# Zero rows under the first products and dummy products between them, in a fused mLSTM and mixture-of-experts kernel

## The chip, the core and the metric

The kernel runs on one core of one Trainium2 chip. Its engines work side by side, each through its own list of instructions in order: TensorE (PE in the profile; PEld is its weight load), VectorE (DVE), ScalarE (ACT), GpSimd (POOL) and SyncE (SP, which here only issues DMAs). The metric is the time on the device in microseconds (us), the median of several runs; lower is better.

## What is computed

An mLSTM attention over 4 batches, 8 heads, 768 positions and head size 40, then a dense layer with a squared ReLU, then a layer in which each token goes to one of 8 experts:

```python
# attention, for each step t (k, v, q of that step; gates i and f)
m_new  = maximum(f + m, i)
f_stab = exp(f + m - m_new);  i_stab = exp(i - m_new)
C = f_stab * C + i_stab * (v k^T);  n = f_stab * n + i_stab * k
y[t] = sigmoid(o) * (C q) / maximum(|n . q|, 1)
# x: 3072 tokens of 320, from y
x = maximum(x @ w_in, 0)**2 @ w_out                       # w_in 320 x 2048
# expert layer: e = argmax(x @ w_gate), p = softmax(x @ w_gate)[e]
out = p * (maximum(x @ w1[e], 0) @ w2[e])                 # w1 320 x 1024
```

All of it is float32.

## The kernel before

The 768 positions of each batch are cut into 6 chunks of 128, 24 chunks in all. Within a chunk the recurrence becomes matrix products: scores of keys against queries (`scores`, L743, tiles `sp`), weighted with the decays of the gates (`Ab`) and multiplied with the values (`values`, L752, tiles `pv`), plus the state `C` of the chunks before, read with the queries (`triples`, L708, tiles `tp<-C,q`) and updated with keys and values (tiles `tp<-vw,kvo`). The result is transposed (`across`, L717, tiles `xpt`) and split into a high and a low part (L725 to L727), since the dense layer works with float32 numbers as pairs of a high part that PE multiplies in one pass and a rest. Three chunks make a group of 384 tokens; for each group the dense layer runs over 16 slices `f` of its 2048 columns: eight products into `hp` (`l1`, L817), the squared ReLU on ACT and DVE, nine products into `acc` (`l2`, L846 to L848). The expert layer follows from about 578 us on.

One chunk is a generator, `main(n)`, of eight steps that end with `yield`. Its first six are advanced by the letter `h` of a string, `PLAN` (L62), its last two (transpose and split) by `y`. Other letters of the string load and unpack the weights of the dense layer (`A`, `R`, `T`, `W`, `H`, `L`; on ACT, DVE and POOL, L519 to L570), prepare the next chunk (`q`, `k`, `d`, `x`, `e`, `v`, `r`), advance the gates (`g`) and emit the dense layer (`l`, `s`, `m`). The code runs through the string once; that sets the order of every engine's instructions. The letter `h` stands 20 times ahead of the first `l`, the first products into `hp`; these steps reach into the fourth chunk. `nl[0]` counts the `l` emitted so far.

The gates of all chunks are turned into running sums `A`, on 36 rows (4 batches of 9), by two scans on DVE (`gate_stage`, L457 and L465). For chunk 0 the decays come from PE: `decays_first` adds a mask `neg`, by a product with the identity (L641), and then, head by head, row `2h + j` of `A`, picked out by a product with a matrix `sel` of 36 rows (L644). Then `columns` transposes three tables of the gates (L483, tiles `pt`) into `cT`, `wT` and `eAT`. Later chunks get their decays by DMA (L631).

For the first seven chunks (`WHOLE = 7`) keys and queries are loaded as 40 rows each and multiplied as float32, in several passes of PE (each such product has two records in the trace). From the eighth chunk on the product has 120 rows, which hold high and low parts of the same numbers, and one pass. The tiles `st` for them have 120 rows in both cases and rotate through two buffers.

`ones` is a tile of 128x128 bf16 ones that POOL fills at the beginning (L859). `acc0` is the PSUM bank of the dense layer's first accumulator. It is not used before the first `m`.

Of the kernel before, what the change touches and what calls it, by code (L numbers as in the profile page):

```python
# [9 lines left out]
F32 = mybir.dt.float32  # L10
# [7 lines left out]
ACTF = mybir.ActivationFunctionType  # L18
# [5 lines left out]
B, H, S, D = 4, 8, 768, 40  # L24
L = 128
NCH = S // L
HB = H + 1
HR = B * HB
# [24 lines left out]
XC_DVE = 2  # L53
FETCH = 2
PERIOD = 6

WHOLE = 7
KVO = 3
# [307 lines left out]

@with_exitstack
def kernel(ctx, tc, qk, q3, kvo, gates, w_in, w_out, wg, w12, cst, out, dbg=None):
    nc = tc.nc
    dbg = dbg or {}  # L370
# [6 lines left out]
    def pool(name, bufs, to, **kw):  # L377
        p = tc.tile_pool(name=name, bufs=bufs, **kw)
        to.append(p)
        return p.__enter__()  # L380
# [5 lines left out]
    ps2 = pool("ps2", 1, early_ps, space=PSUM)  # L386
# [4 lines left out]
    ident = cs[:, 0:128]  # L391
# [22 lines left out]
    xt = ctx.enter_context(tc.tile_pool(name="xt", bufs=2))  # L414
# [3 lines left out]
    at1 = pool("at1", 1, brief, side="right")  # L418
    at2 = pool("at2", 2, brief, side="right")
# [14 lines left out]
    def gate_stage():  # L434

        fi = scr[0:HR, 0:2 * S]
        nc.sync.dma_start(out=fi, in_=gates)
        f, i = fi[:, 0:S], fi[:, S:2 * S]

        sel = at1.tile([120, 2, H * L], F32, tag="kq", name="sel")[0:HR, 0].rearrange("p (h l) -> p h l", h=H)  # L440
        neg = at1.tile([128, H, 42], F32, tag="Y", name="neg").rearrange("p h d -> p (h d)")[:, 0:L]
        m = xt.tile([HR, S + 1], F32, tag="xh", name="m")
        a = xt.tile([HR, S], F32, tag="xh", name="a")
        A = xt.tile([HR, S], F32, tag="xl", name="A")
        c = xt.tile([HR, S], F32, tag="xl", name="c")
        msk = xrl.rearrange("p t n -> p (t n)")[0:HR, 0:S]
        wv, eA = msk, a
        yield
        nc.gpsimd.memset(msk, 1.0)
        nc.gpsimd.memset(msk.rearrange("p (c l) -> p c l", l=L)[:, :, 0:1], 0.0)  # L450
        nc.vector.memset(m[:, 0:1], -1e30)
        nc.gpsimd.memset(neg, 0.0)
        nc.gpsimd.affine_select(out=neg, in_=neg, pattern=[[1, L]], compare_op=ALU.is_ge, fill=-1e30, base=0, channel_multiplier=-1)
        nc.scalar.activation(out=sel, in_=ident[0:HR, 0:H].rearrange("p (h o) -> p h o", o=1).to_broadcast([HR, H, L]), func=ACTF.Copy)
        chunks[0].rows = (sel, neg, A)
        yield
        nc.vector.tensor_tensor_scan(out=m[:, 1:], data0=f, data1=i, initial=-1e30, op0=ALU.add, op1=ALU.max)  # L457
        yield
        nc.vector.tensor_tensor(out=a, in0=f, in1=m[:, 0:S], op=ALU.add)
        nc.gpsimd.tensor_tensor(out=c, in0=i, in1=m[:, 1:], op=ALU.subtract)  # L460
        yield
        nc.vector.tensor_tensor(out=a, in0=a, in1=m[:, 1:], op=ALU.subtract)
        nc.vector.memset(a[:, 0:1], 0.0)
        yield
        nc.vector.tensor_tensor_scan(out=A, data0=msk, data1=a, initial=0.0, op0=ALU.mult, op1=ALU.add)  # L465
        A3 = A.rearrange("p (c l) -> p c l", l=L)

        nc.sync.dma_start(out=A_d, in_=A)
        yield
        nc.vector.tensor_tensor(out=c, in0=c, in1=A, op=ALU.subtract)  # L470
        nc.scalar.activation(out=eA, in_=A, func=ACTF.Exp)
        yield
        nc.vector.tensor_tensor(
            out=wv.rearrange("p (c l) -> p c l", l=L),
            in0=c.rearrange("p (c l) -> p c l", l=L),
            in1=A3[:, :, L - 1:L].to_broadcast([HR, NCH, L]),
            op=ALU.add,
        )

        def columns(src, dst):  # L480
            pt = psa.tile([128, 512], F32, tag="a", name="pt")
            for ch in range(NCH):
                nc.tensor.transpose(out=pt[:, HR * ch:HR * ch + HR], in_=src[:, L * ch:L * ch + L], identity=ident[0:HR, 0:HR])  # L483
            nc.scalar.activation(out=dst, in_=pt[:, 0:HR * NCH].rearrange("p (c h) -> p c h", h=HR), func=ACTF.Copy)

        columns(c, cT)
        yield
        nc.scalar.activation(out=wv, in_=wv, func=ACTF.Exp)
        columns(wv, wT)
        yield  # L490
        columns(eA, eAT)
        eAL = const.tile([HR, NCH], F32, name="eAL")
        nc.vector.tensor_copy(out=eAL.rearrange("p (c o) -> p c o", o=1), in_=eA.rearrange("p (c l) -> p c l", l=L)[:, :, L - 1:L])
        nc.gpsimd.dma_start(out=L_d, in_=eAL)
        yield
# [88 lines left out]
    where = [divmod(n, 3) for n in range(NC)]  # L584
    first = [sum(GROUPS[:g]) for g in range(len(GROUPS) + 1)]
    xT = {}

    class Chunk:

# [13 lines left out]

        def qk(self):

            self.st = []
            for j in range(2):
                st = at2.tile([120, H * L], F32, tag="st", name="st")
                rows = D if self.n < WHOLE else 3 * D
                nc.sync.dma_start(out=st[0:rows], in_=qk[self.b, self.c, j, 0:rows])  # L610
                self.st.append(st)
            if self.c > 0:
                self.q3 = at2.tile([120, 3, L], F32, tag="q3", name="q3")
                nc.sync.dma_start(out=self.q3.rearrange("p g l -> p (g l)"), in_=q3[self.b, self.c])
# [19 lines left out]
        def decays_first(self):  # L634
            sel, neg, A = self.rows
            self.Ab = []
            self.Ap = []
            for j in range(2):
                self.Ab.append(at4.tile([128, 4, L], F32, tag="Ab", name="Ab"))
                self.Ap.append(psa.tile([128, 4, L], F32, tag="a", name="Ap"))  # L640
                nc.tensor.matmul(self.Ap[j], ident, neg.rearrange("p (o l) -> p o l", o=1).to_broadcast([128, 4, L]), start=True, stop=False)  # L641
            for j in range(2):
                for h in range(4):
                    nc.tensor.matmul(self.Ap[j][:, h], sel[:, 2 * h + j], A[:, 0:L], start=False, stop=(h == 3))  # L644
# [25 lines left out]
    chunks = [Chunk(n) for n in range(NC)]  # L670
# [19 lines left out]
    def ahead(m, name, *a):  # L690
        if (m, name, *a) not in over:
            over.add((m, name, *a))
            assert name != "decay" or m == 0 or (m, "causal", *a) in over
            log.append(LETTER[name])
            getattr(chunks[m], "decays_first" if (name, m) == ("decays", 0) else name)(*a)

    def more(name):

        for m in range(NC):
            for j in ((0,), (1,)) if name in ("causal", "decay", "round") else ((),):  # L700
                if name == "round" and m < WHOLE or (m, name, *j) in over:
                    continue
                return ahead(m, name, *j)
# [25 lines left out]
    def main(n):  # L729

        d = chunks[n]
        b, c, last = d.b, d.c, d.last
# [4 lines left out]
        def scores():  # L737
            for r in range(2):
                sps.append(psa.tile([128, 4, L], F32, tag="a", name="sp"))
            for h in range(H):  # L740
                c = slice(L * h, L * h + L)
                k, q = (d.st[j][0:D, c] for j in range(2)) if n < WHOLE else (d.kq[:, j, c] for j in range(2))
                nc.tensor.matmul(sps[h % 2][:, h // 2], k, q, start=True, stop=True)  # L743

        def weigh(r):
# [112 lines left out]
    ones = const.tile([128, 128], BF16, name="ones")  # L858
# [225 lines left out]
    def step():  # L1084
        n = steps[0] // PERIOD
        if n < NC:
            log.append("h")
            next(mains[n])
        steps[0] += 1

    def rest():

        n = tails[0]
        if n < NC and steps[0] >= PERIOD * (n + 1):
            log.append("y")
            if next(mains[n], "end") == "end":
                tails[0] += 1
# [14 lines left out]
    def evac(n):  # L1112

        return PERIOD * n + 8

    def half(n):

        if steps[0] < evac(n):
            n, h = divmod(steps[0], PERIOD)
            rest()  # L1120
            step()
            prepare(n, h)
# [5 lines left out]
    with tc.manual_schedule():  # L1128
# [4 lines left out]
        nl, nd = [0], [0]  # L1133
# [185 lines left out]
            letters[x] = lambda x=x: turn(x)  # L1319
        for name, x in LETTER.items():  # L1320
            letters[x] = lambda name=name: more(name)
        for word in PLAN:
            for x in word:
                if x in "tBS":
                    {"t": lambda: tick(1), "B": lambda: half(NC), "S": settle}[x]()
                else:
                    if x in "gcz":
                        log.append(x)
                    letters[x]()
        if ALL:  # L1330
            dbg.setdefault("log", []).append("".join(log))
# [135 lines left out]
```

## Time and profile before

| | |
|---|---|
| median of 3 runs | 792.76 us (791.84 to 796.58) |
| the profiled execution | 796.21 us, of which the span of its instructions 794.3 |
| PE busy | 745.2 us (94% of the span) |
| DVE, ACT, POOL busy | 506.8, 434.7, 362.2 us |
| chain of work that ended last, by engine | PE 76%, DVE 9%, DMA 5%, ACT 4%, issue 3%, POOL 1% |
| granted TensorE clock, mean over the span | 0.993 |

Busy times are sums over one engine. An engine's record of a product lasts from its start to its end in the array, and neighbours overlap, so a row's time for several is that of the whole run of them. The granted clock is the share of 2.4 GHz that the records of the clock tell of: 1.00 is 2.4 GHz, 0.50 is 1.2. The idle time in square brackets in a timeline row is that of the engine just before the row.

### The profile page before, as it was taken

The numbers are of one execution on the slowest core, as the hardware profiler recorded it, in microseconds if no ns is written. First come the engines' busy times: TensorE is split into PE (matmuls) and PEld (weight loads), VectorE is DVE, ScalarE is ACT, GpSimd is POOL, SyncE is SP. The second block draws the span as 40 slices with busy tenths as digits, with TensorE's granted clock in tenths as the row PEclk, the third lists the DMA queues.
The fourth block names the chain that finished last, engine by engine and source line by source line (L and its number), as shares of the span: only waits on it lengthen the run. The fifth ranks groups of instructions, "written<-read, shape, count | busy, mean of one in ns | idle before, by whom it ended". The sixth has DMA issues, their size and how long they took to land.

```text
span 794.3 us, 14262 instructions
## 1 busy us (share of the span) xinstructions
PE 745.2 (94%) x5075; PEld 730.6 (92%) x5075; DVE 506.8 (64%) x1169; ACT 434.7 (55%) x811; POOL 362.2 (46%) x430
## 2 busy tenths in 40 slices
PE   5676999999999999999999999999979999999996
PEld 3675999999999999999999999999979999999995
DVE  4674787677766677676568755363647555867553
ACT  5877796544653544553544543544246555866453
POOL 2775356554763455364345300423126444556640
PEclk9999999999999999999999999999999999999998
DMA  7575556444654445344345000100168665875620
GB/s 224 154 219 179 168 170 175 139 128 144 215 158 133 114 114 145 104 113 144 113 114 166 7 1 32 32 31 1 61 227 275 185 173 169 250 234 192 200 82 15
DMA packets 58822, 109.29 MB, mean 138 GB/s; under 512 B 7132, under 2 KB 36413, under 8 KB 58614
## 3 DMA queue, kind: packets, MB, share of 16 engines
q1 hardware_dynamic: 49542, 84.67, 36.6%
q10 hardware_dynamic: 5040, 11.82, 4.8%
q0 software_dynamic: 4160, 11.77, 4.5%
q8 instruction: 46, 0.75, 0.4%
q14 instruction: 34, 0.28, 0.1%
HBM read 99.37 MB, written 10.50 MB: 138 GB/s over the span
## 4 chain that ended last, share of the span: by engine, by line
PE 76%; DVE 9%; DMA 5%; ACT 4%; issue 3%; POOL 1%; ACTq 0%; SPq 0%; DVEq 0%; POOLq 0%
PE hp L817 21%; PE hp L282 12%; PE acc L846 6%; PE acc L848 6%; PE acc L847 6%; PE pv L752 4%; PE op L302 4%; PE op L301 4%; PE op L303 4%; DMA st<-in_qk_dram 3%; PE sp L743 2%; PE tp L708 2%; DMA raw<-in_w_in_dram 2%; PE lp L911 2%; PE xp L268 1%
## 5 line engine op out<-in xcount | busy, mean ns | idle before, releaser
L624 POOL TENSOR_TENSOR kq<-st,kq 120x256 fp32r<-120x256 f32 x136 | 96.4, 743 | 66.8 <-ACT kq L621 66.8
L846 PE MATMUL acc<-wo_h,gh 128*128 128x320 f32 x384 | 124.7, 325 | 0.0
L848 PE MATMUL acc<-wo_h,gl 128*128 128x320 f32 x384 | 119.0, 310 | 0.4 <-DVE gl L833 0.4
L847 PE MATMUL acc<-wo_l,gh 128*128 128x320 f32 x384 | 118.5, 309 | 0.0
L817 PE MATMUL hp<-xh,win_h 128*128 128x384 f32 x384 | 114.0, 351 | 4.2 <-DVE xh L727 2.4
L825 ACT ACTIVATE g<-hp 128x384 f32<-128x384 f32 x128 | 62.1, 486 | 92.7 <-PE hp L817 88.2
L832 DVE SCALAR_TENSOR_TENSOR hp<-hp,g 128x384 f32<-128x384 f32 x128 | 71.5, 559 | 56.8 <-ACT g L825 56.5
L251 DVE SCALAR_TENSOR_TENSOR gl<-hp,gh 128x384 fp32r<-128x384 f32 x88 | 47.1, 553 | 71.1 <-ACT gh L221 68.2
L817 PE MATMUL hp<-xh,win_l 128*128 128x384 f32 x384 | 88.1, 337 | 0.0
L817 PE MATMUL hp<-xl,win_h 128*128 128x384 f32 x256 | 87.4, 342 | 0.0
L833 DVE TENSOR_TENSOR gl<-hp,gh 128x384 fp32r<-128x384 f32 x128 | 71.4, 558 | 14.1 <-ACT raw L527 0.5
L848 PEld LDWEIGHTS acc<-wo_h,gl 128*128 128x128 f32 x384 | 72.3, 188 | 0.6 <-DVE gl L833 0.6
L847 PEld LDWEIGHTS acc<-wo_l,gh 128*128 128x128 f32 x384 | 72.6, 189 | 0.0
L846 PEld LDWEIGHTS acc<-wo_h,gh 128*128 128x128 f32 x384 | 72.5, 189 | 0.1
L817 PEld LDWEIGHTS hp<-xh,win_h 128*128 128x128 f32 x384 | 66.4, 191 | 5.8 <-issue 1.8
L826 ACT ACTIVATE gh<-g 128x384 fp32r<-128x384 f32 x128 | 67.2, 525 | 7.8 <-PE acc L847 4.0
L817 PEld LDWEIGHTS hp<-xh,win_l 128*128 128x128 f32 x384 | 69.6, 190 | 0.0
L221 ACT ACTIVATE gh<-hp 128x384 fp32r<-128x384 f32 x88 | 42.5, 491 | 44.5 <-PE hp L282 41.2
L621 ACT ACTIVATE kq<-st,cs 120x1024 fp32r<-120x1024 f32 x34 | 38.9, 1146 | 49.0 <-DMA st<-in_qk_dram 49.0
L752 PEld LDWEIGHTS pv<-kvo,Ab 128*128 128x128 f32 x384 | 52.9, 208 | 11.7 <-issue 5.5
L752 PE MATMUL pv<-kvo,Ab 128*128 128x42 f32 x384 | 52.0, 291 | 10.7 <-DVE Ab L747 9.2
L658 ACT ACTIVATE Ab<-Ab 128x512 f32<-128x512 f32 x46 | 29.0, 631 | 50.8 <-POOL Ab L653 50.1
(265 smaller groups left out, 1853.5 us busy)
## 6 DMA issues: line engine op xcount, KB each, us to landing
st<-in_qk_dram SPq DMA_DIRECT2D x34, 480.0 KB
raw<-in_w_dram SPq DMA_DIRECT2D x30, 512.0 KB
kvo<-in_kvo_dram SPq DMA_DIRECT2D x24, 529.0 KB
Ab<-A_d SPq DMA_DIRECT2D x46, 256.0 KB
raw<-in_w_dram SPq DMA_DIRECT2D x20, 427.0 KB
raw<-in_w_in_dram ACTq DMA_DIRECT2D x16, 384.0 KB
raw<-in_w_out_dram ACTq DMA_DIRECT2D x16, 320.0 KB
raw<-in_w_dram SPq DMA_DIRECT2D x10, 426.0 KB
```

The source lines that it names most:

```text
L251: e.scalar_tensor_tensor(out=gl[:, j], in0=hp[j % 4], scalar=0.0, in1=gh[:, j].bitcast(F32), op0=ALU.max, op1=ALU.subtract).then_inc(sGL, 1)
L282: m = e.matmul(hp[f % 4][:, 0:w], a, c, start=(n == 0), stop=(n == 7))
L624: nc.gpsimd.tensor_tensor(out=o[:, c], in0=self.st[j][:, c], in1=o[:, c].bitcast(F32), op=ALU.subtract)
L752: nc.tensor.matmul(pv[:, hd], d.Ab[r][:, i], d.v[:, hd], start=True, stop=True)
L817: nc.tensor.matmul(hp, a, x, start=(n == 0), stop=(n == 7))
L825: nc.scalar.activation(out=r, in_=hp, func=ACTF.Relu)
L826: nc.scalar.activation(out=gh, in_=r, func=ACTF.Square)
L832: nc.vector.scalar_tensor_tensor(out=hp, in0=hp, scalar=0.0, in1=r, op0=ALU.max, op1=ALU.mult)
L833: nc.vector.tensor_tensor(out=gl, in0=hp, in1=gh.bitcast(F32), op=ALU.subtract)
L846: nc.tensor.matmul(acc[t][:, 0:DM], gh[:, sl], wh, start=(f == 0), stop=False)
L847: nc.tensor.matmul(acc[t][:, 0:DM], gh[:, sl], wl, start=False, stop=False)
L848: nc.tensor.matmul(acc[t][:, 0:DM], gl[:, sl], wh, start=False, stop=end)
```

## The change

Three things change. First, all products of the early chunks that had 36 or 40 rows get 120, and what is in the further rows is zero: the two `st` tiles of the first seven chunks are allocated once (`padded`) and cleared by DVE at the very beginning, the DMA goes on writing rows 0 to 39 of them, and the products read all 120; `A` and `sel` get 120 rows in the same way, for which DVE clears 128 columns of `A`. Second, `fillers(n)` multiplies the tile `ones` with itself, `n` times 512 columns in bf16, into the bank of `acc0`; nobody reads the result. Ten of these come at the very beginning of PE's list, with 51 products of one column behind them, and eight in `decays_first`, between the mask and the rows of `A`. Third, each `h` ahead of the first `l` emits three of them first, 60 in all.

```diff
+APART = 51
+WARM = 10
+FILL = 3
...
-        sel = at1.tile([120, 2, H * L], F32, tag="kq", name="sel")[0:HR, 0].rearrange("p (h l) -> p h l", h=H)
+        sel = at1.tile([120, 2, H * L], F32, tag="kq", name="sel")[:, 0].rearrange("p (h l) -> p h l", h=H)
...
-        A = xt.tile([HR, S], F32, tag="xl", name="A")
+        A0 = xt.tile([120, S], F32, tag="xl", name="A")
+        A = A0[0:HR]
...
+        for x in padded:
+            nc.vector.memset(x, 0.0)
         yield
+        nc.vector.memset(A0[:, 0:L], 0.0)
...
-        nc.scalar.activation(out=sel, in_=ident[0:HR, 0:H].rearrange("p (h o) -> p h o", o=1).to_broadcast([HR, H, L]), func=ACTF.Copy)
-        chunks[0].rows = (sel, neg, A)
+        nc.scalar.activation(out=sel, in_=ident[0:120, 0:H].rearrange("p (h o) -> p h o", o=1).to_broadcast([120, H, L]), func=ACTF.Copy)
+        chunks[0].rows = (sel, neg, A0)
...
+    padded = [at2.tile([120, H * L], F32, tag="st", name="st") for _ in range(2)]
...
-            self.st = []
+            self.st = padded if self.n < WHOLE else [at2.tile([120, H * L], F32, tag="st", name="st") for _ in range(2)]
+            rows = D if self.n < WHOLE else 3 * D
             for j in range(2):
-                st = at2.tile([120, H * L], F32, tag="st", name="st")
-                rows = D if self.n < WHOLE else 3 * D
-                nc.sync.dma_start(out=st[0:rows], in_=qk[self.b, self.c, j, 0:rows])
-                self.st.append(st)
+                nc.sync.dma_start(out=self.st[j][0:rows], in_=qk[self.b, self.c, j, 0:rows])
...
+            self.fillers(8)
             for j in range(2):
                 for h in range(4):
                     nc.tensor.matmul(self.Ap[j][:, h], sel[:, 2 * h + j], A[:, 0:L], start=False, stop=(h == 3))
...
-                k, q = (d.st[j][0:D, c] for j in range(2)) if n < WHOLE else (d.kq[:, j, c] for j in range(2))
+                k, q = (d.st[j][:, c] for j in range(2)) if n < WHOLE else (d.kq[:, j, c] for j in range(2))
...
+        apart = ps2.tile([128, 512], F32, tag="acc0", name="apart")
+
+        def fillers(n):
+
+            for _ in range(n):
+                nc.tensor.matmul(apart, ones, ones.rearrange("p (o n) -> p o n", o=1).to_broadcast([128, 4, 128]), start=True, stop=True)
+
+        chunks[0].fillers = fillers
+        fillers(WARM)
+        for _ in range(APART):
+            nc.tensor.matmul(apart[:, 0:1], ones, ones[:, 0:1], start=True, stop=True)
...
+                    if x == "h" and not nl[0]:
+                        fillers(FILL)
                     letters[x]()
```

The order of the work changes on PE alone, and there only by what is put in between. The beginning of PE's list before, from the mask to the transposed tables of the gates and the first scores:

```order
L641 MATMUL Ap<-neg,cs 128x512 x2
L644 MATMUL Ap<-A,sel 128x128 x8
L483 MATMUL pt<-cs,c 128x36 x6
L483 MATMUL pt<-cs,xrl 128x36 x6
L483 MATMUL pt<-cs,a 128x36 x6
L743 MATMUL sp<-st 128x128 x8
```

The same list now, where the last of the 51 small products meet the mask and the first of the eight dummies (each is a weight load and a product; `apart` is the bank they write):

```order
L1339 LDWEIGHTS ones
L1339 MATMUL apart<-ones 128x1
L647 MATMUL Ap<-neg,cs 128x512 x2
L1334 LDWEIGHTS ones
L1334 MATMUL apart<-ones 128x512
```

Ahead of the mask now stand 61 products, and behind it eight before `Ap<-A`.

The values of the first chunk before, with the state's update ahead of them and the second chunk's state product behind them:

```order
L708 MATMUL tp<-vw,kvo 120x126 x3
L752 MATMUL pv<-kvo,Ab 128x42 x8
L708 MATMUL tp<-C,q_279 128x126 x3
L743 MATMUL sp<-st 128x128 x8
```

The same values now; the four of the first half and the four of the second are two steps of the chunk, with three dummies between them:

```order
L759 MATMUL pv<-kvo,Ab 128x42 x4
L1334 LDWEIGHTS ones
L1334 MATMUL apart<-ones 128x512
L1334 LDWEIGHTS ones
L1334 MATMUL apart<-ones 128x512
L1334 LDWEIGHTS ones
L1334 MATMUL apart<-ones 128x512
L759 MATMUL pv<-kvo,Ab 128x42 x4
```

In the same way six dummies stand between `sp` and `tp<-vw,kvo` and six between the second half of `pv` and `tp<-C,q`, since two letters `h` follow each other there without a product of their own. In the last part before `hp`, three stand ahead of the transpose `xpt`, three between it and `tp<-C,q`, and three between `sp` and the first product into `hp`.

## Rows read from the trace of the kernel before

**Rows 1.** The page, busy tenths in 40 slices of the span: PE.

```profile
PE   5676999999999999999999999999979999999996
```

**Rows 2.** Windows: stretch, length, busy us (instructions) by engine, granted clock, DMA share, GB/s.

```profile
11.50:73.10 61.60, 41.92 (x191) 39.47 (x191) 37.65 (x69) 44.60 (x87) 36.13 (x39) 1.00 0.66 191
...
24.60:29.70 5.10, 0.00 (x0) 0.00 (x0) 2.57 (x4) 3.25 (x8) 4.67 (x6) 1.00 0.73 160
...
59.70:65.70 6.00, 0.00 (x0) 0.00 (x0) 4.77 (x15) 5.71 (x11) 1.86 (x4) 1.00 0.87 269
80.00:160.00 80.00, 79.05 (x551) 77.65 (x551) 59.91 (x131) 56.57 (x110) 41.85 (x59) 1.00 0.59 165
```

**Rows 3.** Timeline of PE before 91 us: start, us, engine, line, tiles, shape, count.

```profile
4.93 3.75 PE L641 MATMUL Ap<-neg,cs 128*128 128x512 f32 x4 [4.93 <-DMA cs<-in_cst_dram]
...
18.74 3.76 PE L743 MATMUL sp<-st 40*128 40x128 f32 x16
...
39.34 0.88 PE L717 MATMUL xpt<-cs,kvo 128*128 128x128 f32 x3 [0.81 <-DVE kvo L793]
...
47.10 1.94 PE L752 MATMUL pv<-kvo,Ab 128*128 128x42 f32 x8 [4.02 <-DVE Ab L747]
...
73.14 0.98 PE L817 MATMUL hp<-xh,win_h 128*128 128x384 f32 x2 [1.50 <-DVE xh L727]
...
75.83 0.59 PE L817 MATMUL hp<-xh,win_h 128*128 128x384 f32 x2
...
87.32 2.05 PE L743 MATMUL sp<-st 40*128 40x128 f32 x16
```

**Rows 4.** Chain of work that ended last, by time: start, us, what, records.

```profile
11.51 3.75 PE Ap L644 x16
15.26 0.61 PE pt L483 x6
...
17.43 0.87 PE pt L483 x6
...
29.79 3.63 PE pv L752 x16
...
61.15 3.80 DMA raw<-in_w_in_dram
...
65.74 0.90 PE xpt L717 x3
66.64 1.28 PE tp L708 x6
67.92 3.30 PE sp L743 x14
...
73.14 5.71 PE hp L817 x24
...
83.99 1.41 PE hp L817 x8
```

**Rows 5.** Windows before and behind a fall of the granted clock, columns as above.

```profile
233.00:236.40 3.40, 2.26 (x22) 1.97 (x21) 2.65 (x7) 2.66 (x6) 3.33 (x7) 1.00 0.00 0
236.40:239.80 3.40, 3.40 (x14) 3.40 (x13) 3.23 (x10) 0.87 (x2) 3.33 (x6) 0.50 0.33 77
```

**Rows 6.** Timeline of PE near 236 us: small bf16 products and what follows.

```profile
235.72 0.19 PE L978 MATMUL pr<-oh,tri 128*128 128x24 bf16 x1
...
235.89 0.39 PE L846 MATMUL acc<-wo_h,gh 128*128 128x320 f32 x1
```

**Rows 7.** Groups by line and shape on PE, 0 to 72 us: busy us, mean ns.

```profile
L743 PE MATMUL sp<-st 40*128 40x128 f32 x64 | 15.1, 427 | 0.0
...
L708 PE MATMUL tp<-vw,kvo 128*120 128x126 f32 x18 | 4.7, 433 | 0.5 <-POOL vw L668 0.5
```

**Rows 8.** Timelines of DVE and POOL at the start.

```profile
4.41 1.75 DVE L457 TENSOR_TENSOR_SCAN m<-scr 36x768 f32<-36x768 f32 x1 [3.54 <-DMA scr<-in_gates_dram]
...
0.75 0.20 POOL L859 MEMSET ones<- 128x128 bf16 x1 [0.29 <-POOLq L1456]
```

## The prediction

> **What bounds the kernel now.** I read the page first. In its 40 slices PE is at 9 tenths nearly throughout from the fifth slice on, and at 5, 6, 7 and 6 in the first four [rows 1]. The windows view puts numbers to it: PE is busy 79.05 of 80 us between 80 and 160 us, but 41.92 of 61.60 between 11.5 and 73.1 [rows 2]. From the first product of the dense layer on (hp, 73.14 us) PE is the bound and its order is fixed, so what is saved ahead of that moment is saved at the end, and what is lost there is lost.
>
> Next I read the clock. The column PEclk says 1.00 between 11.5 and 73.1 us [rows 2], but the durations do not: the 16 records of one chunk's scores (sp) take 3.76 us at 18.74 us and 2.05 us at 87.32 [rows 3]. That is the ratio of the two levels, 1.2 and 2.4 GHz, less what small products cost at any clock. The hp products show the step itself: the first eight take 2.69 us (73.14 to 75.83), eight later ones 1.41 [rows 3, 4]. So the column has nothing to tell before about 76 us, and PE ran at 1.2 GHz until then. [...]
>
> What did PE do before its clock moved? It rose some 2.9 us after hp products of 384 columns began. It had not risen through sp (40 of the array's 128 rows), tp and pv before: 14 records of the last sp before hp still take 3.30 us [rows 4]. It fell at 236.4 us, to 0.50, after 3.4 us in which PE was busy for 2.26 [rows 5].
>
> Last the chain of waits before 76 us [rows 4]. It is no PE chain alone: it goes through landings of weights (one is 3.80 us long), ACT's and DVE's unpacking of them, and these PE pieces: Ap 3.75, pt 0.61 and 0.87, pv 3.63, xpt 0.90, tp 1.28, sp 3.30 and hp 5.71, together 20.05 us. Only these can shrink, at best to 0.54 of it (2.05 by 3.76).
>
> **The change, part by part.**
>
> *Prices.* No row shows a bf16 product of 512 columns. From hp's eight, scaled by 512/384: 0.235 us at the high level (1.41/8 x 1.33) and 0.448 at the low one (2.69/8 x 1.33). The four records of Ap<-neg, of 512 columns in two passes each, agree with the latter: 3.75 us, 0.47 a pass [rows 3]. So three dummies are 0.70 or 1.35 us. For a 1-column product the nearest rows are the small bf16 ones: six start within 0.17 us (235.72 to 235.89), 28 ns each at the high level [rows 6]; I bound by 28 and 56.
>
> *Rows and memsets: nothing.* A product's time does not follow its rows: records of 40 rows take 427 ns, of 128 rows 433 [rows 7]. The memsets lie on DVE, which waits 3.54 us for the gates before its first scan [rows 8]; at DVE's rate there (768 columns in 1.75 us at worst) the two of 1024 columns take under 4.7 us, at a column a ns 2. The first score DMA is held up by that long, but the scores are read at 18.74 us. Should the worst case hold, the scan starts about 1.5 us late, which is the cost without that cover; I take none.
>
> *The start.* `ones` is ready at 0.95 us [rows 8]. Ten dummies at 0.448 end at 5.4; the 51 small ones (1.4 to 2.9 us) end at 6.8 to 8.3; then Ap<-neg (3.75, or 2.0) and eight dummies (3.6, or 1.9) stand before Ap<-A, which could start at 11.51. If the clock rises within the first ten, as it did within 2.9 us of hp, PE is there by 10.7 to 12.2; if only in the second dense run, at about 14. Ap<-A then takes 2.0 instead of 3.75, and the pt steps on the chain half of 1.48. ACT waits for exactly these, so this gives 1.7 + 0.7 = **2.4 us** with PE on time, and nothing with PE late.
>
> *First values (pv at 29.79).* PE waits 5.10 us here with nothing in it [rows 2]. Six dummies stand ahead of tp and three behind it, all at the beginning of the wait; then 4 to 5 us stay empty. By rows 5 I take the clock as fallen. Then pv keeps its 3.63 us, and three dummies at 1.35 us lie bare between its halves. Of the 2.4 us **1.1** are left. (At the high level: 1.7 less 0.7 more, 3.4 in all, of which I take DVE to pass on 3.0, since its unpacking there waits for ACT.)
>
> *From pv to xpt.* PE has six dummies (2.7 or 1.4), tp (1.6 or 0.8) and sp (3.76 or 2.05) to do while DVE and ACT take 5.9 us from pv's end, 33.42, to xpt at 39.34 [rows 3, 4]. This is a dense stretch, and I take the clock to come back in the middle of it: about 6.2 us, **even**; 2.2 us lost if it stays low. In the second chunk the same two things follow, a wait of 4.02 us before pv at 47.10 [rows 3] and a dense stretch. There only pv's second half stands behind the wait: **+0.5**.
>
> *The last leg (65.74).* PE waits 6.00 us empty [rows 2]; then xpt, tp and sp lead straight to hp, 5.48 us on the chain. High level: 3.0 + 0.7 for the dummies, 1.8 gained. Low: 5.48 + 1.35, 1.35 lost. I take a return of the clock part of the way: **+0.2**.
>
> *hp.* 24 records take 5.71, three times 1.41 is 4.23. Three dummies stand in the 1.50 us wait before them [rows 3], so the clock is back earlier: **+1.2** of 1.48.
>
> Sum: 1.1 + 0 + 0.5 + 0.2 + 1.2 = **3.0 us**. The profiled execution took 796.21 us (span 794.3, 1.9 around it), 3.4 over the median of 792.76 of three runs from 791.84 to 796.58. The stretch is the same in all of them, so I take the 3.0 off the median: **789.8 us**.
>
> If all the time before 76 us were on the path, half of PE's 45.67 busy us (41.92 and Ap's 3.75) would be 22.8; by the chain, with everything at the high level, it is 3.0 + 0.5 + 1.8 + 1.4 = 6.7 us. The Trainium skill (TensorE: Matmul & The Clock Gate, Part 1) says that in modelling the cost of a clock that starts low is under 1% of a usual kernel's span, which would put the gain under 7.9 us; the chain agrees with it, the busy time alone would not.
>
> **The rivals.**
>
> *The clock stays high from the start to hp.* For it: dummies come in 20 steps between 18.74 and 73.14 us, one step each 2.7 us. Against it: empty waits of 5.10 and 6.00 us, which get longer as PE gets faster, and a fall after much less in rows 5. Time: 792.76 - 6.7 = 786.1. If the landings on the chain move up too, two or three us more, 784: over 1%.
>
> *The gain is given back.* Weights are unpacked for the later steps of the dense layer at ACT's and the DMA's pace (DMA share 0.66 from 11.5 to 73.1 us [rows 2]); an earlier hp may find them not there. Against it: in 80 to 160 us PE idles only 0.95 us in all, so the unpacking has some lead now. Time: 791.8 to 794.
>
> *The dummies become the bound (slower).* If the clock stays low, PE gets 60 dummies in steps (27 us), 18 at the start (8.1) and 51 small ones (2.9): 38 us. Up to 73.14 PE had 73.14 - 45.67 = 27.5 us idle. So hp comes some 10.5 us later, **803**. With the clock low in about half of the stretch PE is late at xpt and hp by 1 to 4 us: 794 to 797. It decides where the low share of the dummies passes what the waits hold. Against the full loss: a dense run of 512-column products is more of what raised the clock at 76 us, not less.
>
> *The rows don't do what they are there for.* The clock rises with the dummies but sp does not hold or raise it, if rows of zeros do not count. That changes the last leg by 1 to 2 us, which lies in the forecast's own range.
>
> **How the numbers follow.** Clock up and down as summed, 787.8 to 791.8: 0.5. Clock high throughout: 0.2, of which 0.10 below 784.8. Gain given back, or none of it there: 0.17. Dummies in the way: 0.13, of which 0.07 above 800.7. A measurement of this kernel tells about 1% (7.9 us) from no change. So faster 0.10, same 0.83, slower 0.07. The range, 785.5 to 795.5, leaves about 0.1 out on each side; it holds the bounds of the small products (1.5 us), of late memsets (1.5) and of late dummies at Ap (2.4).
>
> **What would show it.** sp's 16 records near 2 us instead of 3.76, and for which chunks; Ap<-A starting at 11.5 or later; slow records of pv after the waits at about 27, 45 and 64 us; hp's first product at 70 to 72 us instead of 73.14. I am wrong if the clock holds through the long waits (then about 786), or if PE has no idle time left before hp (then over 795).

## The result and the profile after

| | before | after |
|---|---|---|
| median of 9 runs each, taken side by side | 792.13 us (790.90 to 796.58) | 800.21 us (798.54 to 805.92) |
| ratio, 95% interval | | 1.0103 [1.0073, 1.0133] |
| the profiled execution, its span | 796.21, 794.3 | 802.33, 800.4 |
| first product into `hp` | 73.14 us | 81.07 us |
| last product into `acc` | 576.4 us | 584.8 us |
| granted clock, mean over the span | 0.993 | 0.973 |

The kernel is 1.0% slower, 8.1 us by the medians. The forecast was 789.8 us within 785.5 to 795.5, so it is missed on the slow side. The loss is there before the dense layer begins: `hp` starts 7.9 us later, and the last `acc` ends 8.4 us later. The two figures of the granted clock can't be compared: before's counts its first 76 us as 1.00, where the durations are those of 1.2 GHz [rows 3], while after's records tell of the clock from 5.6 us on. In 41 of the 81 runs of the kernel before that stand beside the experiments the mean is 0.947 to 0.957, in the others 0.986 to 0.999.

The timeline of PE after the change, from the start to `hp`, shows where (columns as in [rows 3]; `apart` are the dummies):

```profile
1.00 4.45 PE L1334 MATMUL apart<-ones 128*128 128x512 bf16 x10 [1.00 <-POOL ones L866]
5.24 1.48 PE L1339 MATMUL apart<-ones 128*128 128x1 bf16 x51
6.58 1.96 PE L647 MATMUL Ap<-neg,cs 128*128 128x512 f32 x4
8.38 1.89 PE L1334 MATMUL apart<-ones 128*128 128x512 bf16 x8
12.22 3.60 PE L651 MATMUL Ap<-A,sel 120*128 120x128 f32 x16 [1.95 <-DVE A L472]
...
19.63 3.39 PE L750 MATMUL sp<-st 120*128 120x128 f32 x16
...
29.97 1.91 PE L759 MATMUL pv<-kvo,Ab 128*128 128x42 f32 x8 [4.36 <-DVE Ab L754]
...
41.75 3.75 PE L750 MATMUL sp<-st 120*128 120x128 f32 x16 [3.18 <-DMA st<-in_qk_dram]
...
61.90 3.76 PE L750 MATMUL sp<-st 120*128 120x128 f32 x16 [5.37 <-DMA st<-in_qk_dram]
...
81.07 0.59 PE L824 MATMUL hp<-xh,win_h 128*128 128x384 f32 x2 [1.05 <-ACT wo_h L572]
```

Two waits are new. The scores of the second and of the third chunk wait 3.18 and 5.37 us, and what they wait for is the landing of `st`, the keys and queries. Before the change no `sp` waits for a DMA; the same two then (no idle time ahead of either):

```profile
34.75 3.78 PE L743 MATMUL sp<-st 40*128 40x128 f32 x16
50.39 3.78 PE L743 MATMUL sp<-st 40*128 40x128 f32 x16
```

PE's waits, summed by what ended them (until 85 us; total, times, longest), first after and then before:

```profile
PE sp L750 <- DMA st<-in_qk_dram: 8.6, 2, 5.4
PE pv L759 <- DVE Ab L754: 5.9, 2, 4.4
PE xpt L724 <- DVE kvo L800: 2.1, 1, 2.1
```

```profile
PE pv L752 <- DVE Ab L747: 9.2, 2, 5.2
PE xpt L717 <- DVE kvo L793: 6.9, 2, 6.1
```

The chain of waits after the change runs through those landings, and through two more in the fifth and sixth chunks, which come after the start of `hp`:

```profile
35.66 5.95 DMA st<-in_qk_dram
41.75 3.75 PE sp L750 x16
...
54.02 7.79 DMA st<-in_qk_dram
61.90 3.76 PE sp L750 x16
...
89.28 6.71 DMA st<-in_qk_dram
96.13 1.81 PE sp L750 x14
...
110.84 5.76 DMA st<-in_qk_dram
```

Why a load ends a wait that was not there shows in what SP waits for. These are waits of its DMAs, until 85 us (total, times, longest), first before and then after; L610 and L617 load `st`, L637 the decays `Ab`:

```profile
SPq L610 <- PE sp L743: 28.3, 4, 11.0
```

```profile
SPq L617 <- PE sp L750: 14.2, 2, 7.6
SPq L637 <- PE pv L759: 13.8, 6, 4.1
```

In that time SP loads `st` four times behind the first, before and after. Before, each of the four waits for scores. Now the second and the fifth chunk's do (issued at 23.05 and 79.40 us), the third and the fourth chunk's (35.23 and 53.58) do not. In `PLAN` the letter `q` that loads the next chunk stands ahead of the `h` that emits the scores of the present one, for the chunks 1, 2, 4 and 5 (counted from 0, so the second, third, fifth and sixth). As long as every chunk allocates its tile `st`, the load goes into a new tile that takes the old one's place, and waits until the scores have read the old one. With the pair `padded` allocated once there is one tile for all chunks, and the order of the code alone says who comes first: the load is written, then the scores read, so the scores wait for the landing.

The scores of these four chunks then multiply the next chunk's keys and queries instead of their own. So the changed kernel no longer computes what stands under "What is computed". Shapes and amount of work are the same, so its time can still be compared; in E4 and E8 below the scores read their own chunk.

SP's timeline says why that landing is late. The load is issued only behind `Ab<-A_d`, the decays of the same chunk, which themselves wait for PE's products with the values (`pv`):

```profile
31.95 3.19 SPq L637 DMA_DIRECT2D Ab<-A_d  x2
35.23 0.76 SPq L617 DMA_DIRECT2D st<-in_qk_dram  x2
...
49.83 3.65 SPq L637 DMA_DIRECT2D Ab<-A_d  x2
53.58 0.77 SPq L617 DMA_DIRECT2D st<-in_qk_dram  x2
```

Before, the first of these two loads was issued at 38.56 us, behind the scores of the second chunk (34.75 to 38.53), and nobody was waiting for it.

The granted clock of after, in the windows view (columns as in [rows 2]), goes up and down, as the forecast had it, though not at the same places (`Ap<-A` and the `sp` at 61.90 us run at 0.50):

```profile
5.60:12.30 6.70, 4.75 (x58) 2.53 (x55) 6.46 (x6) 4.60 (x7) 2.84 (x2) 1.00 0.67 218
12.40:15.80 3.40, 3.40 (x17) 3.18 (x16) 2.33 (x4) 1.26 (x2) 0.00 (x0) 0.50 0.76 219
...
22.70:29.40 6.70, 2.91 (x18) 1.65 (x17) 3.93 (x3) 4.07 (x11) 6.55 (x8) 1.00 0.84 185
29.50:46.50 17.00, 13.35 (x52) 10.67 (x53) 10.39 (x17) 10.24 (x19) 10.81 (x12) 0.50 0.63 171
...
60.20:67.00 6.80, 5.10 (x20) 4.12 (x21) 1.73 (x4) 2.93 (x6) 4.55 (x6) 0.50 0.33 104
```

The high stretches lie to a good part over the empty waits (in 22.70 to 29.40 us PE is busy for 2.91 of 6.70), the low ones over the work behind them (13.35 of 17.00).

### The profile page after: what moved, and what is told of

Its sections match the earlier page's. It is cut to its first block, busy times and chain, and to the rows that moved or that the text cites. A ratio compares the mean times of both kernels' runs of the same rounds, so it can differ in the third digit from the quotient of the medians.

```text
span 800.4 us, 14514 instructions
## 1 busy us (share of the span) xinstructions
PE 755.5 (94%) x5204; PEld 729.9 (91%) x5204; DVE 510.7 (64%) x1172; ACT 434.6 (54%) x811; POOL 362.0 (45%) x430
## 4 chain that ended last, share of the span: by engine, by line
PE 74%; DVE 10%; DMA 7%; ACT 3%; issue 3%; POOL 1%; SPq 1%; DVEq 0%; ACTq 0%; POOLq 0%
PE hp L824 20%; PE hp L285 11%; DMA st<-in_qk_dram 6%; PE acc L853 6%; PE acc L855 6%; PE acc L854 6%; PE pv L759 4%; PE op L305 3%; PE op L304 3%; PE op L306 3%; PE sp L750 3%; PE tp L715 2%; PE lp L918 1%; PE xp L271 1%; PE xpt L724 1%
## 5 line engine op out<-in xcount | busy, mean ns | idle before, releaser
L630 POOL TENSOR_TENSOR kq<-st,kq 120x256 fp32r<-120x256 f32 x136 | 96.2, 740 | 66.4 <-ACT kq L627 62.8
L824 PE MATMUL hp<-xh,win_l 128*128 128x384 f32 x384 | 87.5, 335 | 0.0
L759 PEld LDWEIGHTS pv<-kvo,Ab 128*128 128x128 f32 x384 | 50.2, 197 | 9.2 <-issue 4.8
L759 PE MATMUL pv<-kvo,Ab 128*128 128x42 f32 x384 | 48.9, 279 | 6.9 <-DVE Ab L754 5.9
```

What stands on the lines that cost most here:

```text
L630: nc.gpsimd.tensor_tensor(out=o[:, c], in0=self.st[j][:, c], in1=o[:, c].bitcast(F32), op=ALU.subtract)
L759: nc.tensor.matmul(pv[:, hd], d.Ab[r][:, i], d.v[:, hd], start=True, stop=True)
L824: nc.tensor.matmul(hp, a, x, start=(n == 0), stop=(n == 7))
```

## The experiments

All ratios are to runs of the kernel before in the same job, with 95% intervals. E1 to E4 were run on one chip, E5 to E8 on a second, E9 to E12 on a third.

**E1, the shared tiles alone.** The kernel before, with nothing but the two tiles allocated once:

```diff
+    padded = [at2.tile([120, H * L], F32, tag="st", name="st") for _ in range(2)]
...
-                st = at2.tile([120, H * L], F32, tag="st", name="st")
+                st = padded[j] if self.n < WHOLE else at2.tile([120, H * L], F32, tag="st", name="st")
```

> The kernel before with one edit: the two st tiles of the first seven chunks are allocated once and used by every chunk; products keep 40 and 36 rows, no memsets, no dummies. The scores of chunks 1, 2, 4 and 5 then read the keys and queries of the next chunk, since the load of the next chunk stands ahead of them in the code. Theory S (the shared tiles are the cause): scores wait for the landing of the next chunk's load, as they do in the changed kernel's trace (sp at 41.75 and 61.90 us, against 34.75 and 50.39 before); PE is at 1.2 GHz throughout the beginning, so hp starts 8 to 11 us late (81 to 84 us, before 73.14) and the time is 800 to 803 us. Theory D (the dummies stand in the way of real products): as before, 791 to 793 us, hp at 73.

Measured: 809.32 us, ratio 1.0240 [1.0199, 1.0281]. Two lines of code, no dummy and no further row, lose 17 us, more than the whole change does, and about twice what had been expected of them. The waits are there at the same places:

```profile
39.53 3.75 PE L745 MATMUL sp<-st 40*128 40x128 f32 x16 [5.42 <-DMA st<-in_qk_dram]
...
59.30 3.75 PE L745 MATMUL sp<-st 40*128 40x128 f32 x16 [6.01 <-DMA st<-in_qk_dram]
...
79.20 0.98 PE L819 MATMUL hp<-xh,win_h 128*128 128x384 f32 x2 [1.50 <-DVE xh L729]
...
97.83 3.05 PE L745 MATMUL sp<-st 40*128 40x128 f32 x16 [3.03 <-DMA st<-in_qk_dram]
```

`hp` starts 6.1 us late. The rest is lost behind that: the first group of the dense layer, from its first `hp` to the next group's, takes 69.9 us instead of 60.1. (The two profiled executions took 807.57 and 796.21 us, so these starts do not add up to the difference of the medians.) The waits of the fifth and sixth chunks are one part of it (PE idles 4.8 us there instead of 0.9), and behind each of them the clock is at 0.50 for a while; these are low windows of E1 behind the two waits:

```profile
98.60:105.40 6.80, 6.44 (x26) 6.15 (x25) 4.72 (x10) 3.19 (x7) 2.61 (x3) 0.50 0.27 80
...
122.50:125.90 3.40, 3.40 (x13) 3.18 (x11) 3.31 (x5) 3.25 (x7) 3.32 (x4) 0.50 0.34 96
```

**E2, the dummies alone.** The change without the shared tiles and without the further rows:

```diff
-            self.st = padded if self.n < WHOLE else [at2.tile([120, H * L], F32, tag="st", name="st") for _ in range(2)]
+            self.st = [at2.tile([120, H * L], F32, tag="st", name="st") for _ in range(2)]
...
-                k, q = (d.st[j][:, c] for j in range(2)) if n < WHOLE else (d.kq[:, j, c] for j in range(2))
+                k, q = (d.st[j][0:D, c] for j in range(2)) if n < WHOLE else (d.kq[:, j, c] for j in range(2))
```

> The change without its first part: products keep 40 and 36 rows, st tiles are allocated per chunk as before, no memsets; all 78 dummies of 512 columns and the 51 of one column are there. Theory S: the loads wait for the scores as before, so the time is what was predicted for the whole change or a little less gain, 788 to 792 us, hp at 69 to 73 us. Theory D: still slower than before, 797 to 801 us, hp at 78 to 81 us.

Measured: 793.40 us, ratio 1.0011 [0.9983, 1.0040]. The dummies do not cause the loss. `hp` comes at 70.49 us, 2.65 earlier in this one profile (E7 and E11 below show how far such a start scatters), and the profile shows how the lead went: behind the next scores, still of 40 rows, the clock falls, and the first group takes 61.9 us instead of 60.1. In the kernel before the clock did not fall behind the same scores (1.00 from 80 to 160 us [rows 2]). Two windows of E2, on either side of that:

```profile
84.10:87.50 3.40, 2.88 (x24) 2.57 (x22) 1.71 (x5) 0.88 (x2) 2.86 (x7) 1.00 0.42 153
87.60:90.90 3.30, 3.30 (x12) 3.30 (x13) 3.12 (x8) 2.38 (x5) 3.06 (x5) 0.50 0.79 173
```

**E3, shared tiles and further rows, no dummies.**

```diff
-            self.fillers(8)
...
-        fillers(WARM)
-        for _ in range(APART):
-            nc.tensor.matmul(apart[:, 0:1], ones, ones[:, 0:1], start=True, stop=True)
...
-                    if x == "h" and not nl[0]:
-                        fillers(FILL)
```

> The change without any dummy: shared st tiles, cleared once, products of 120 rows with zeros. The scores of chunks 1, 2, 4 and 5 read the next chunk's keys and queries, as in the change. Theory S: as the shared tiles alone, 800 to 803 us. Theory D: 791 to 794 us. If the zero rows alone raise the clock, the sp records take 2 us somewhere before 73 us; I expect 3.7 us for all of them before hp.

Measured: 802.70 us, ratio 1.0131 [1.0098, 1.0163]; `hp` at 78.66. The waits for `st` are as in E1 (5.74 and 6.31 us), yet it is 6.6 us ahead of E1, and the intervals lie apart: the rows of zeros are worth that much where the waits are. In E3's profile the clock rises five times before 76 us (at 8.4, 15.2, 22.0, 45.9 and 66.4) and again at 76.6, in E1's once (9.8). With the dummies on top, the whole change, the ratio is 1.0103; the intervals overlap.

**E4, the whole change with the loads late.** Four letters `q` of `PLAN` (and a `d`) moved behind the `h` that emits the scores; nothing else. The line of `PLAN` with the first of the places (`dHqHTLRexWhL` to `dHHTLRexWhqL`):

```diff
-    AAAqggkggTTRsPRgdWHAgWAgHgPReRWRggxHvWALhAkHTdWehxARxTqcsvshsLxTWhHPLARRhheWAdHqHTLRexWhLxkyWyhMdALAHLyRHTRQLWyTWyAHhAhL
+    AAAqggkggTTRsPRgdWHAgWAgHgPReRWRggxHvWALhAkHTdWehxARxTqcsvshsLxTWhHPLARRhheWAdHHTLRexWhqLxkyWyhMdALAHLyRHTRQLWyTWyAHhAhL
```

> The whole change, but the letter q of PLAN that loads the next chunk stands behind the h that emits the scores of the chunk before it (four letters moved, and one d behind one of them so that SP's DMAs keep the order they had before the change). Each load then waits for the scores that read the tiles, and the scores read their own chunk. Theory S: the loss is gone, 788 to 792 us, hp at 69 to 73 us, no wait of sp for an st landing. Theory D: 797 to 801 us, as the change. Against the dummies without the zero rows it also tells what the rows do to the clock: sp's 16 records at 2 us in more places, or not.

Measured: 789.40 us, ratio 0.9976 [0.9955, 0.9997]. The whole loss is gone and a small gain is left. This is the one edit that isolates the cause within the change. The moved letters put the loads where the kernel before has them anyway: there each is issued right behind the scores that read the old tile (at 38.56, 54.20 and 71.67 us; those scores end at 38.53, 54.17 and 71.63). So the letters should be worth nothing by themselves; no run has them moved in the kernel before. PE's timeline of E4 has no wait for `st`:

```profile
27.90 1.90 PE L759 MATMUL pv<-kvo,Ab 128*128 128x42 f32 x8 [4.40 <-DVE Ab L754]
29.60 1.49 PE L1334 MATMUL apart<-ones 128*128 128x512 bf16 x3
30.87 1.77 PE L759 MATMUL pv<-kvo,Ab 128*128 128x42 f32 x8
32.44 2.77 PE L1334 MATMUL apart<-ones 128*128 128x512 bf16 x6
35.00 1.49 PE L715 MATMUL tp<-C,q 120*128 120x126 f32 x6
36.28 2.31 PE L750 MATMUL sp<-st 120*128 120x128 f32 x16
...
70.96 0.59 PE L824 MATMUL hp<-xh,win_h 128*128 128x384 f32 x2 [1.06 <-DVE xh L734]
```

**E8, the other way out: a second pair of tiles.** The letters stay as in the change, and odd chunks get a pair of their own, so that a load never writes what the scores ahead of it still read:

```diff
+        nc.gpsimd.memset(scr[0:120, 0:2048], 0.0)
...
+    pads = [padded, [scr[0:120, 1024 * j:1024 * j + 1024] for j in range(2)]]
...
-            self.st = padded if self.n < WHOLE else [at2.tile([120, H * L], F32, tag="st", name="st") for _ in range(2)]
+            self.st = pads[self.n % 2] if self.n < WHOLE else [at2.tile([120, H * L], F32, tag="st", name="st") for _ in range(2)]
```

> The whole change with the letters in their old order, but chunks of odd number load into a second pair of tiles (in scr, which is free between the gates and the first group's end, cleared on GpSimd). Scores read their own chunk, and a load waits for the scores of the chunk before the last instead of the last. Theory S: no wait of sp for a landing, as the late load, 787 to 790 us; since the loads come 10 us earlier and no longer block SP's queue, some of it could be better than the late load. If the earlier loads collide with weight loads in the DMA: up to 2 us worse than the late load.

Measured: 791.88 us, ratio 0.9987 [0.9963, 1.0011], `hp` at 71.31. No `sp` waits for a load here either, and the loss is gone: E4's result does not hang on the letters. The time is 1.9 us above the range expected of it.

**E7 and E11, the further rows alone with the loads late** (E4 without any dummy, the lines taken out as in E3). E11 repeats E7 beside its neighbours.

> The zero rows alone: late loads, no dummy anywhere. In the run with zero rows and shared loads the clock rose six times before 76 us, with 40 rows and shared loads once, at 9.8. If the rows by themselves raise the clock enough to be worth something: 789 to 791 us. If they need the dummies: 792 to 794 us, with all sp records before hp at 3.4 to 3.8 us.

> Zero rows and late loads without any dummy, again, as the common base of this job. Both theories: ratio 0.994 to 0.998, hp near 70.4 us.

Measured: 789.22 us, ratio 0.9957 [0.9936, 0.9978], and 790.71 us, ratio 0.9964 [0.9942, 0.9985]. `hp` starts at 70.43 in one profile and at 72.99 in the other, so a single start of `hp` is good to some 2.5 us. Rows of zeros, which compute nothing, gain about 0.4%. (A run with the shared tiles, the late loads and 40 rows was not made; the pair that differs by the rows and their memsets alone is E1 and E3.) Four of E7's windows show how:

```profile
40.30:53.90 13.60, 10.12 (x47) 9.97 (x48) 10.62 (x22) 11.62 (x22) 8.69 (x9) 0.50 0.73 225
54.00:60.70 6.70, 3.23 (x27) 2.83 (x25) 5.85 (x10) 5.89 (x12) 6.24 (x7) 1.00 0.84 221
60.80:67.60 6.80, 3.56 (x17) 3.56 (x18) 4.58 (x12) 5.10 (x10) 3.08 (x3) 0.50 0.74 249
67.70:133.00 65.30, 62.29 (x432) 60.93 (x431) 48.92 (x104) 50.99 (x99) 37.41 (x51) 1.00 0.59 172
```

The clock rises at 53.9 us, just before the scores at 50.61 end, and again at 67.6 in the middle of the next scores (66.02 to 68.73), ahead of `hp`. In the kernel before it did neither, and rose only some 2.9 us into `hp`.

**E6 and E9, the start's dummies on top** (the 18 dummies and the 51 small ones at the beginning, none in the steps). E9 repeats E6. To E4:

```diff
-FILL = 3
+FILL = 0
```

> The late load without the 60 dummies in the steps; the 10 and 51 at the start, the 8 in the decays and the zero rows stay. By the prediction's sum the start alone is worth 2.4 us up to the first pv, and what lies behind it 0.5 to 2: 790 to 792 us, the clock low from about 25 us to hp. If the start is worth nothing: 792 to 793.

> The same kernel as in the run with late loads, zero rows and the dummies of the start alone (no dummies in the steps), now on one chip beside its two neighbours. Theory N (the zero rows hold the clock, dummies in the steps add nothing): within 0.3% of the kernel with zero rows and late loads alone, ratio to before 0.992 to 0.997. Theory W (the dummies of the start are worth their own 2.4 us): 0.3% ahead of that kernel, ratio about 0.993.

Measured: 788.49 us, ratio 0.9931 [0.9903, 0.9958], and 788.59 us, ratio 0.9938 [0.9917, 0.9959]. That is 0.26% ahead of the further rows alone in both jobs; the intervals overlap, so it is likely rather than shown. E6 is 1.5 us below the range expected of it.

**E10, the steps' dummies on top of E7** (E4 without the start's):

```diff
-            self.fillers(8)
...
-        fillers(WARM)
-        for _ in range(APART):
-            nc.tensor.matmul(apart[:, 0:1], ones, ones[:, 0:1], start=True, stop=True)
```

> Zero rows, late loads and the 60 dummies in the steps, no dummies at the start. Theory N: the steps' dummies add nothing to the zero rows, and where PE is late they cost, so the ratio to before is that of the zero rows alone (0.9957) or up to 0.3% worse. Theory U (the steps' dummies shorten the stretch by themselves): ahead of the zero rows alone by 0.2% or more, and hp starts ahead of 70.4 us.

Measured: 792.39 us, ratio 0.9990 [0.9971, 1.0008], against 0.9964 for the further rows alone on the same chip. The 60 dummies in the steps seem to cost rather than gain; the intervals overlap.

**E5 and E12, dummies in the long waits.** E5 adds 16, 8 and 22 dummies to E4 at three steps, ahead of the values of the first chunk, of the second half of the second chunk's values and of the third transpose; E12 has these without the 60 of the steps:

```diff
+MORE = {3: 16, 10: 8, 17: 22}
...
-                        fillers(FILL)
+                        fillers(FILL + MORE.get(steps[0], 0))
```

> The late load (the whole change with each load behind the scores that read its tiles), with more dummies at the three steps behind which PE still waits longest in its trace: 16 more ahead of pv of chunk 0 (wait 4.40 us), 8 more ahead of the second half of pv of chunk 1 (2.33 us), 22 more ahead of the transpose before hp (5.70 us). At 0.22 us each they fit the waits if the clock is high: 3.5, 1.7 and 4.8 us. Theory C (the falls of the clock in the long waits cost what is missing of the gain): pv of chunk 0 takes 1.0 us a half instead of 1.9 and 1.77, xpt, tp and sp before hp run at the high level, hp starts 2 to 3 us earlier, 786 to 788 us where the late load has 789.4. Theory N (the weights' unpacking bounds that stretch, PE is hidden there): within 1 us of the late load. Theory D (dummies in the way): the waits vanish and hp is later, 791 us or more.

> Zero rows, late loads, the dummies of the start, and dummies only in the three long waits of PE (16, 8 and 22 of 512 columns ahead of the values of the first and second chunk and of the third transpose), none in the other steps. Theory N: hp moves up to about 67.5 us, as in the kernel that had these and the 60 others, and the median follows by what hp gains, 2 us ahead of the start alone (ratio 0.990 to 0.993). Theory G (the gain ahead of hp is given back later, since the unpacking sets the pace): hp near 67.5 us but the median no better than with the start alone.

Measured: E5 791.20 us, ratio 0.9960 [0.9935, 0.9985], `hp` at 67.39. E12 786.17 us, ratio 0.9911 [0.9883, 0.9940], `hp` at 65.57, the best version here, 7.4 us ahead of before by the medians. In E5 `hp` comes 3.6 us ahead of E4's, as its theory C had it, but the median does not follow (786 to 788 expected); where that lead goes, and whether E5's other executions have it, stays open. The timeline of E12 ahead of `hp`:

```profile
53.87 4.92 PE L1335 MATMUL apart<-ones 128*128 128x512 bf16 x22
60.86 0.55 PE L725 MATMUL xpt<-cs,kvo 128*128 128x128 f32 x3 [2.07 <-DVE kvo L801]
...
61.91 1.95 PE L751 MATMUL sp<-st 120*128 120x128 f32 x16
65.57 0.58 PE L825 MATMUL hp<-xh,win_h 128*128 128x384 f32 x2 [1.70 <-DVE xh L735]
```

Here the 6.00 us wait of [rows 2] holds 22 dummies, nothing behind it is slow any more, and `xpt` to `hp` takes 4.71 us instead of 7.40. E5 against E12, E4 against E6 and E9, and E10 against E7 and E11 differ by the steps' dummies alone: 0.5, 0.4 and 0.3%, each time on the slow side. The intervals of each pair overlap, and only E10 and E11 ran on one chip, so that these dummies cost is likely, not shown.

## Why the prediction was wrong, by its own steps

**The failing step is "Rows and memsets: nothing", and with it the sentence that the order of the work changes on PE alone.** It put the shared tiles at 0; measured are the new waits of 3.18 and 5.37 us, and `hp` 7.9 us later instead of 1.8 earlier. The part asked what a product with more rows costs and what the memsets cost, and both answers held (sp's 16 records last 3.75 us at the low level with either number of rows; the memsets of the two tiles take 0.91 us each and are done before the gates land). It never asked what "allocated once" does. The allocation of a tile is also a wait: with it went SP's wait for the scores, and in its place came the scores' wait for the load. SP issues its DMAs in the same order in both timelines; what they wait for is not the same. That was to be had before the run, and so was a first estimate of the price: SP's issue of the load stands behind `Ab<-A_d`, and the landing took some 6 us from there (35.66 to 41.61 on the chain). None of the rivals had it. The sign named for a time over 795, that PE has no idle time left before `hp`, did not show: PE stood idle for 8.6 us, waiting for `st`. E1 shows that it alone makes the loss, E4 and E8 that the change without it loses nothing.

With that wait taken out (E4), the rest of the prediction can be read step by step:

| step | predicted, gained by then | E4's profile against [rows 3, 4] |
|---|---|---|
| Prices: a dummy high, low; a small one | 0.235, 0.448; 28 to 56 ns | 0.236 (1.89 for 8), 0.46 (2.77 for 6); 29 ns (1.48 for 51, in after) |
| The start, at `pv` | 2.4 us | 27.90 for 29.79: 1.9 |
| First values, at their end | 1.1 | 32.64 for 33.42: 0.8 |
| From `pv` to `xpt` | 1.1 | 38.67 for 39.34: 0.7 |
| Second chunk's second half | 1.6 | 45.59 for 47.10 at its start: 1.5; 46.68 for 49.04 at its end: 2.4 |
| The last leg, at `hp` | 1.8 | 70.96 for 73.14: 2.2 |
| `hp`, 24 products | 1.2 | 4.43 (in after, and in E4) for 5.71: 1.3 |
| Sum, time | 3.0, 789.8 us | ratio 0.9976: 1.9 us (0.2 to 3.6), 2.9 by the medians; 789.40 us |

So the rest of the working agrees with E4 as far as one profile can tell. A start of `hp` scatters by some 2.5 us between executions (E7, E11), so an agreement within 1 us in one row, and the 0.4 us between 789.8 and 789.40, are in part luck. The clock went up and down where it was expected to: fallen in the wait ahead of the first `pv` (1.90 and 1.77 a half, with the three dummies at 1.49 bare between them), back in the dense stretch behind it.

**The start** did not hold in after's own profile. The clock had risen right behind the first ten dummies, at 5.6 us (Ap<-neg takes 1.96 us instead of 3.75), but `A` came 0.7 us later than before, and by the end of PE's wait of 1.95 us for it the clock had fallen, so that Ap<-A took 3.60 us. In the seven other profiles with these dummies (E2, E4 to E6, E8, E9, E12) it took 2.02, and `pv` starts 1.6 to 2.9 us ahead of before. So the 2.4 us were about right, and after's profile is the exception. The 0.7 us lie in the scatter: Ap<-A starts at 11.43 to 12.25 us in E1 to E12.

**"What is saved ahead of `hp` is saved at the end"** held roughly for E12, 7.6 us early at `hp` and 7.4 ahead by the medians. After is 7.9 us late at `hp` and 8.1 by the medians, but this is in part luck: the loads in the fifth and sixth chunks cost more, and the next group's first `hp` is 10.0 us late (143.23 for 133.27). It failed where the clock falls behind `hp`: E2 (2.65 early, nothing at the end), and E1 (6.1 late, 17.1 behind at the end). For E5 (5.75 early, by its ratio 3.2 ahead, 1.2 to 5.2) it is open.

**The rivals.** "The rows don't do what they are there for" was wrong: E7 and E11 gain by them alone, and in none of the nine profiles of E4 to E12 did the clock fall in the first group of the dense layer. With 40 rows it fell there in E1 and E2, but not in the kernel before, and in E3 it fell with 120 rows too, at 93.7 us in a wait for `st`; so that the rows hold the clock there is likely, not shown. "The clock stays high" was not what the change does, but E12 comes near it: its 786.2 us stands beside the 786.1 of that rival, by chance, since its dummies lie elsewhere and its clock is still low from 16.1 to 22.8 and from 29.8 to 50.1 us. "The gain is given back" is what E2 shows at the end, but not for that rival's reason: PE idles 0.94 us in E2's first group, as before (0.95), so the weights were there, and the clock fell. "The dummies become the bound" did not come true: its price, 803, is near the result by chance, for the dummies alone are at 1.0011. In E4 they lie on the path at one place, where pv, late, is followed by six of them at the low clock: from the start of `pv` to `sp` it is 8.4 us (27.90 to 36.28), in E7 without dummies 4.8 (29.80 to 34.62). The lead of 1.9 us is used up there.

The Trainium skill (TensorE: Matmul & The Clock Gate, Part 1) puts, for modelling, a clock that starts low at under 1% of a usual kernel's span. The runs agree within their noise: the most that any version here got is 0.9% (E12, 0.6 to 1.2 by its interval), with the clock still low in part of the stretch.

What stays open is the split of the last 0.5%: that the start's dummies are worth 0.26% and the long waits' another 0.27% comes from ratios whose intervals overlap.

## What to carry to other kernels

When a tile that was allocated for every use becomes one tile for all, compare the two programs with their waits, not the order alone: the pool's wait of the writer for the last reader goes, and each load that stands ahead of a reader in the code becomes something the reader waits for, and what it then reads is that load's data. Look then at what stands ahead of that load in its DMA queue, since that sets the length of the wait. In these runs dummy products seem to pay where PE is empty for several us (E12); between steps in which PE may be late they are work on the path (E4, from `pv` to `sp`).

## What the runs showed of the hardware

Rows of zeros, which add nothing to the result and next to nothing to a product's time (sp's 16 records take 3.75 us with 120 rows and 3.76 with 40 at the low level, 1.95 and 2.05 at the high one), changed the granted clock. With waits for `st` of about the same length and no dummy it rose once before 76 us with 40 rows (E1) and five times with 120 (E3), and E3 is 6.6 us faster. In E7, without any dummy, it rose from 0.50 to 1.00 at 53.9 us and again at 67.6, in scores of 120 rows. In the kernel before it was still low in the last scores of 40 rows ahead of `hp` [rows 4]. In E2 it fell at 87.5 us behind scores of 40 rows, with PE busy for 2.88 of the 3.40 us ahead of the fall; in the kernel before it did not fall behind the same scores. The prediction gave the rows no gain of their own.

A load that comes late can cost more than its wait: in E1 the waits of 3.03 and 1.06 us for `st` in the dense layer were each followed by a stretch at 0.50, 6.8 and 3.4 us long, in which a product of 384 columns took 0.52 us instead of 0.34. In after, with 120 rows, the waits of 2.09 and 1.20 us at the same places were not followed by a fall.
